# Attention stage of a three-stage kernel: nine tile buffers instead of five, row stores issued by ScalarE, four weight units loaded at the stage's end

## The chip, the cores and the metric

One core of one Trainium2 chip runs the whole program. The metric is device time in microseconds of one execution. A profiled execution gives the trace from which all rows below come; three timed runs give the median.

## The reference

Three layers follow each other. Inputs are float32.

```python
# 1 retention-like attention, batch 8, heads 8, sequence 576, head size 64
ret = (q @ k.T) / 8 * gamma_h ** (i - j) * (i >= j)
x = (ret @ v), laid out as 4608 tokens x 512
# 2 mixture of experts, 8 experts, one expert per token (argmax of x @ w_gate)
h = relu(xe @ w1[e]);  ye = h @ w2[e];  out[mask] = softmax_weight * ye
# 3 dense layer
g = relu(x @ w_in) ** 2;  result = g @ w_out
```

## The kernel before, in words

The kernel works through three stages in an order that is written out by hand; each engine takes its own instructions in that order. The change is in the first stage alone.

**Attention stage.** The 4608 tokens are cut into 36 tiles of 128 tokens. Nine tiles make a pair of batches: tiles 0 to 3 are the four 128-token chunks of one batch, 4 to 7 those of the next, and tile 8 holds the last 64 tokens of both (`kind`). For each tile `load` (L364) brings one array of 128 partitions x 4 x 512 floats (q, k, v and k again: 1 MB; 0.75 MB for every ninth tile) into one of five buffers of the pool `in_p`. In the loop over t, `load(t + 4)` is issued first, so its buffer is the one that tile t-1 has just left. Then, for tile t:

- `scores(t + 1)`: TensorE multiplies k by q (L387), VectorE masks the result into `r` (L393).
- `scale_v(t + 2)`: GpSimd scales v by a table (L374).
- `fold` and `logits` (L476, L467), each in every second tile: the gate's logits of a pair of tiles. ScalarE copies them out of PSUM (L471).
- `out_x(t)`: TensorE multiplies the chunk state `sts` by q (L435; not for the first chunk of a batch; for the ninth tile L428 twice as often) and `r` by v (L439). VectorE scales the sum by the table `tabx` (L447) and transposes it in blocks of 32 into one of three buffers `xr` (L449).
- `state(t)`: TensorE adds v times k to the chunk state (L411), ScalarE copies it to `sts` (L418); the next tile's L435 reads it.

The rows of x go to DRAM (`x_d`) by `put` (L456): four stores of 64 KB each, in pieces of 512 bytes. `out_x(t)` only notes `put` in the list `late`; it is issued in loop t+1, right behind that loop's load, on the same queue (SyncE's, SP):

```python
for t in range(NT):
    ready, late[:] = late[:], []
    if t + 4 < NT:
        load(t + 4)
    ...
    for f in ready:
        f()
```

In the loops t = 12, 18, 24 and 30 SP also issues `load_unit` (L107): one unit of weights of expert 0, 0.5 MB, into the one buffer `stg`. Two loops later `split_unit` makes its high part on ScalarE (L113) and its low part on GpSimd (L115), in a buffer of the pool `w_a`, which has four buffers of 8 KB per partition. These four units are used right behind the attention stage.

Beside this, `group` makes each token's place in its expert's list from the logits of a group of tiles, in steps that `todo` hands out one per loop. After the third group two rows of places are known; GpSimd gathers those 256 rows of x (`lead`, L270), and in the loops 33 and 34 `lead_turn` transposes them on TensorE (L286) and splits them.

**Behind the loop** come `late` (the last tile's `put`), the loads of the units 4 and 5 in halves (L689), and then TensorE's first work of the second stage: `first(0)` (L806 to L808) on the lead rows, `first(1)`, the last logits, `second(0)` (L830), which needs ScalarE's and VectorE's copies of `first(0)` (L812, L813), and so on while the last group's places are made and GpSimd gathers the rest of expert 0's rows (`xs`). Seven more experts and the dense layer follow.

Of the kernel before, what the change touches and what calls it, by code (L numbers as in the profile page):

```python
# [7 lines left out]
F32 = mybir.dt.float32  # L8
F32R = mybir.dt.float32r
# [10 lines left out]
NT = 36  # L20
NE = 8
CAP = 640
CT = CAP // 128
# [2 lines left out]
NF = 16  # L26
FIN = 6
LEAD = 2
MORE = 6
TINY = 2.0 ** -15 * 1.125  # L30
GROUPS = [(0, 8), (8, 16), (16, 24), (24, 30), (30, 36)]
# [18 lines left out]
def body(ctx, tc, att, tab_v, tab_x, masks, wg, ident, pick, cst, wu, wd, out):  # L50
    nc = tc.nc
    vec, act, pe, pool, sp = nc.vector, nc.scalar, nc.tensor, nc.gpsimd, nc.sync

    def scope(stack, name, bufs, space=None, side=None, reuse=None):
        kw = {"space": space, "side": side, "reuse_waits": reuse}
        kw = {k: v for k, v in kw.items() if v is not None}
        return stack.enter_context(tc.tile_pool(name=name, bufs=bufs, **kw))

    const = scope(ctx, "const", 1)
    xs_p = scope(ctx, "xs_p", 1)  # L60
    xf_p = scope(ctx, "xf_p", 2)
    w_a = scope(ctx, "w_a", 4, side="right")
    pools = {}
# [25 lines left out]
    sidx2 = places.tile([128, NE], I32, name="sidx2")  # L89
    lead_idx = places.tile([128, LEAD], I32, name="lead_idx")  # L90
    oh2 = places.tile([128, NT, 2 * NE], BF16, name="oh2")
# [9 lines left out]
    def ring(u):  # L101
        return w_a if u % 8 < 4 else pools["w_b"]


    def load_unit(u, on=None):
        raw = on.tile([128, CT, 4, 128], F32, tag="xs", name="raw").rearrange("p a b c -> p (a b c)")[:, 0:1024] if on else pools["stg"].tile([128, 1024], F32, tag="raw", name="raw")
        sp.dma_start(out=raw, in_=wu[u])  # L107
        return raw

    def split_unit(u, raw, on):  # L110

        w = ring(u).tile([128, 2, 1024], F32R, tag="w", name="w")
        act.activation(out=w[:, 0], in_=raw, func=AF.Copy)  # L113
        w_q[u] = w
        return lambda: on.tensor_tensor(out=w[:, 1], in0=raw, in1=w[:, 0].bitcast(F32), op=ALU.subtract)  # L115
# [211 lines left out]
    rt_ps = scope(chain, "rt_ps", 1, PSUM, side="right")  # L327
    with ExitStack() as es:
        tabs = scope(es, "tabs", 1)
        pools["stg"] = scope(es, "astg", 1)  # L330
        in_p = scope(es, "in_p", 5)
        sp_p = scope(es, "sp_p", 3)
        r_p = scope(es, "r_p", 2)
# [6 lines left out]
        tabx = tabs.tile([128, 5, 4, 128], F32, name="tabx")  # L340
# [10 lines left out]
        def kind(t):  # L351
            g, c = divmod(t, 9)
            if c == 8:
                return None, 4
            return 2 * g + c // 4, c % 4

        def load(t):
            a = in_p.tile([128, 4, 512], F32, tag="in", name="in")
            n = 3 if kind(t)[1] == 4 else 4
            in_t[t] = a  # L360
            if t < 4:
                sp.dma_start(out=a[:, 0:2], in_=att[t, :, 0:2])
            else:
                sp.dma_start(out=a[:, 0:n], in_=att[t, :, 0:n])  # L364
# [33 lines left out]
        def stslot(b, c):  # L398
            return sts[2 + b % 2] if c == 3 else sts[c % 2]
# [20 lines left out]
        def out_x(t):  # L420
            b, c = kind(t)
            q = in_t[t][:, 0].rearrange("p (h n) -> p h n", h=4)
            ps = x_ps.tile([128, 4, 128], F32, tag="x", name="x")
            if c == 4:
                for i in range(2):
                    s = stslot(i, 3)
                    for p in range(4):
                        pe.matmul(  # L428
                            ps[:, p], s[:, p], zq[:, p, i:i + 2].rearrange("p a n -> p (a n)"),
                            start=(p == 0 and i == 0), stop=False, skip_group_check=True,  # L430
                        )
            elif c > 0:
                s = stslot(b, c - 1)
                for p in range(4):
                    pe.matmul(ps[:, p], s[:, p], q[:, p], start=(p == 0), stop=False, skip_group_check=True)  # L435
            for p in range(4):
                for s in range(2):
                    h = 2 * p + s
                    pe.matmul(  # L439
                        ps[64 * s:64 * s + 64, p], vs_t[t][:, 64 * h:64 * h + 64],  # L440
                        r_t[t, s][:, p],
                        start=(c == 0 and p == 0), stop=(p == 3), skip_group_check=True,
                    )
            if t % 2 == 0:
                xp_t[t // 2] = xp_p.tile([128, 4, 256], F32, tag="x", name="x")
            x = xp_t[t // 2][:, :, 128 * (t % 2):128 * (t % 2) + 128]
            vec.tensor_tensor(out=x, in0=ps, in1=tabx[:, c], op=ALU.mult)  # L447
            xr = xr_p.tile([128, 4, 4, 32], F32, tag="xr", name="xr")
            vec.transpose(  # L449
                out=xr.rearrange("q t k j -> q k t j"), in_=x.rearrange("q k (t i) -> q k t i", i=32)  # L450
            )

            def put():
                rows = x_d[128 * t:128 * t + 128, :].rearrange("(t i) (a c) -> a i t c", i=32, a=4)
                for a in range(4):
                    sp.dma_start(  # L456
                        out=rows[a], in_=xr[32 * a:32 * a + 32].rearrange("q t k j -> q t (k j)")
                    )

            late.append(put)  # L460

        def logits(j):
# [108 lines left out]
        def lead_kept(bank):  # L571
# [4 lines left out]
            vec.tensor_scalar(  # L576
                out=kept, in0=kept, scalar1=-1.0, scalar2=128.0 * (LEAD + 1), op0=ALU.mult, op1=ALU.add
            )
# [3 lines left out]
        def lead_rows():  # L582
            f = rt.tile([128, LEAD], F32, tag="lf", name="lf")
            vec.scalar_tensor_tensor(
                out=f, in0=inv[:, NS:NS + LEAD], scalar=128.0, in1=inv[:, 0:LEAD], op0=ALU.mult, op1=ALU.add
            )
            vec.tensor_scalar(out=lead_idx, in0=f, scalar1=-1.0, scalar2=0.0, op0=ALU.add, op1=ALU.max)
            for i in range(LEAD):
                if not lead_s:
# [4 lines left out]
        def lead_turn(i):  # L594
# [3 lines left out]
            act.activation(out=hi, in_=ps, func=AF.Copy)  # L598
            vec.tensor_tensor(out=lo, in0=ps, in1=hi.bitcast(F32), op=ALU.subtract)

        todo = []
        raw = {}
        lead = pools["cw_p"].tile([128, 4, 512], F32R, tag="cw", name="lead")
        lead_x = [
            lead[:, 2 * s:2 * s + 2].rearrange("p s (k n) -> p (s k) n", n=128 * LEAD) for s in range(2)
        ]
# [28 lines left out]
        fold = None  # L635
        for t in range(NT):
            ready, late[:] = late[:], []
            if t + 4 < NT:
                load(t + 4)
            if t in (1, 2, 4):  # L640
                c = {1: 2, 2: 3, 4: 4}[t]
                sp.dma_start(out=tabx[:, c], in_=tab_x[:, c])
            if t == 0:
                sp.dma_start(out=wg2[:, :, 0:NE], in_=wg)
            if t == 2:
                sp.dma_start(out=idn, in_=ident)
            if t == 4:
                sp.dma_start(out=msk[:, 1], in_=masks[:, 1])
                sp.dma_start(out=cf, in_=cst)
            if t == 6:  # L650
                sp.dma_start(out=sel, in_=pick)
            for f in ready:
                f()
            if t % 6 == 0 and 12 <= t < 36:
                raw[t] = load_unit(t // 6 - 2)
            if t + 1 < NT:
                scores(t + 1)
            if t + 2 < NT:
                scale_v(t + 2)
            if fold:  # L660
                fold()
                for g in GROUPS:
                    if g[1] == t - 2:
                        todo += group(*g)
            fold = logits((t - 3) // 2) if t % 2 and t > 2 else None
            out_x(t)
            state(t)
            if t + 1 < NT:
                spread_q(t + 1)
            if NT - 1 - LEAD <= t < NT - 1:  # L670
                lead_turn(t - NT + 1 + LEAD)
            if todo and t < NT - 1:
                todo.pop(0)()
            if t == 8:
                vec.tensor_copy(ub, cf[:, C_U:C_U + 128])
            if t % 6 == 2 and 12 <= t < 36:
                split_unit(t // 6 - 2, raw.pop(t - 2), pool)()
        for f in late:
            f()
        late.clear()  # L680
# [70 lines left out]
    with ExitStack() as es:  # L751
# [225 lines left out]
        raw, made, wide, last_job = {}, [], [], None  # L977
# [33 lines left out]
        for u in range(NU):  # L1011
# [49 lines left out]
            if u + 1 < NU:  # L1061
                first(u + 1, (1,) if u + 1 < MORE else (0, 1))
            if f == 5:
# [4 lines left out]
            if u < NU - FIN:  # L1068
                second(u, range(LEAD if u < MORE else 0, CT))
                if f == 7:  # L1070
# [32 lines left out]
    with ExitStack() as es:  # L1103
# [213 lines left out]
        def tile_of(T, what, a, b):  # L1317
            return first_of[T] + ((7 * a + KEPT.index(b)) // 4 if what == "up" else 14 + 8 * a + b // 2)
# [50 lines left out]
        for m, (T, what, a, b) in enumerate(slots):  # L1369
# [8 lines left out]
            if what == "up":  # L1378
                up(T, a, b, 512 if T else 256)
                if T < 4 and b in (7, 6) and a in (4, 5):  # L1380
                    if (a, b) == (4, 7):
                        load, jobs = prepare(T + 1)
# [10 lines left out]
            t = tile_of(T, what, a, b)  # L1393
# [85 lines left out]
```

## Time and profile before

| | us |
|---|---|
| median of three runs | 1503.47 (1495.17 to 1505.44) |
| profiled execution, device time | 1493.76 |
| its span in the trace | 1492.0 |
| TensorE busy in the span | 1386.8 (93%) |
| VectorE, ScalarE, GpSimd busy | 827.2, 548.2, 356.6 |

The span is the time from the first to the last instruction. Busy times are sums over instructions; TensorE's are modelled and overlap its waits in part. In the rows below a start and a length are in microseconds from the span's start. SPq and ACTq are the DMA issues of SyncE and ScalarE; a name such as `in<-att` is the tile written and the tensor read. A DMA's length in the chain is the time from its issue to its landing.

### The profile page before, as it was taken

The numbers are of one execution on the slowest core, as the hardware profiler recorded it, in microseconds if no ns is written. First come the engines' busy times: TensorE is split into PE (matmuls) and PEld (weight loads), VectorE is DVE, ScalarE is ACT, GpSimd is POOL, SyncE is SP. The second block draws the span as 40 slices with busy tenths as digits, with TensorE's granted clock in tenths as the row PEclk, the third lists the DMA queues.
The fourth block names the chain that finished last, engine by engine and source line by source line (L and its number), as shares of the span: only waits on it lengthen the run. The fifth ranks groups of instructions, "written<-read, shape, count | busy, mean of one in ns | idle before, by whom it ended". The sixth has DMA issues, their size and how long they took to land.

```text
span 1492.0 us, 21533 instructions
## 1 busy us (share of the span) xinstructions
PE 1386.8 (93%) x8121; PEld 1173.8 (79%) x8121; DVE 827.2 (55%) x1512; ACT 548.2 (37%) x1064; POOL 356.6 (24%) x366
## 2 busy tenths in 40 slices
PE   8888998696969798979999999999999999999998
PEld 6777797595949697969797788888888888788887
DVE  5666756383828585857268446534562447435422
ACT  1222243252415253424255344324442444334321
POOL 2232274525251625431123002200030003100000
PEclk9999998797969898979999999999999999999999
DMA  9999745454526565534676666666675666655563
GB/s 316 311 280 301 213 144 189 128 195 141 194 81 231 171 209 183 203 124 170 245 282 249 216 213 223 223 225 207 201 243 203 218 225 226 214 209 197 197 226 113
DMA packets 107712, 311.02 MB, mean 208 GB/s; under 512 B 20430, under 2 KB 55758, under 8 KB 85584
## 3 DMA queue, kind: packets, MB, share of 16 engines
q1 hardware_dynamic: 97152, 288.15, 56.8%
q0 software_dynamic: 9872, 21.15, 4.7%
q8 instruction: 66, 1.08, 0.3%
q14 instruction: 46, 0.38, 0.1%
q10 hardware_dynamic: 576, 0.26, 0.1%
HBM read 257.98 MB, written 52.58 MB: 208 GB/s over the span
## 4 chain that ended last, share of the span: by engine, by line
PE 72%; DMA 12%; issue 10%; POOL 2%; DVE 2%; SPq 1%; ACT 1%; POOLq 0%; DVEq 0%; ACTq 0%
PE b L1146 22%; PE fa L1214 8%; PE fa L1216 8%; PE fa L1215 8%; DMA in<-att 7%; PE l L807 4%; PE l L806 4%; PE l L808 4%; PE acc L830 4%; PE acc L831 4%; PE acc L832 4%; POOL xs L270 1%; DMA wq<-ws_d 1%; DMA tabx<-tab_x 1%; DMA y_d<-y,sidx 1%
## 5 line engine op out<-in xcount | busy, mean ns | idle before, releaser
L1146 PE MATMUL b<-xt,wq 128*128 128x512 f32 (+1 forms) x1296 | 265.1, 362 | 5.0 <-ACT xt L743 2.3
L1146 PEld LDWEIGHTS b<-xt,wq 128*128 128x128 f32 x1296 | 220.9, 188 | 44.3 <-ACT xt L743 3.0
L1214 PE MATMUL fa<-wq,ch 128*128 128x512 f32 x576 | 224.7, 390 | 2.4 <-DVE fo L1226 1.3
L1216 PE MATMUL fa<-wq,cl 128*128 128x512 f32 x576 | 224.6, 390 | 0.2
L1215 PE MATMUL fa<-wq,ch 128*128 128x512 f32 x576 | 224.2, 389 | 0.0
L1204 DVE TENSOR_TENSOR cl<-g,ch 128x512 fp32r<-128x512 f32 (+1 forms) x160 | 108.4, 687 | 174.2 <-ACT ch L1203 171.8
L734 POOL TENSOR_TENSOR xsum<-yf 128x256 f32<-128x256 f32 x80 | 64.2, 813 | 457.5 <-DVE yf L722 390.5
L807 PE MATMUL l<-xt,w 128*128 128x320 f32 (+1 forms) x480 | 155.0, 323 | 18.7 <-issue 18.6
L808 PE MATMUL l<-xt,w 128*128 128x320 f32 (+1 forms) x480 | 154.4, 322 | 17.0 <-issue 17.0
L806 PE MATMUL l<-xt,w 128*128 128x320 f32 (+1 forms) x480 | 154.2, 321 | 13.5 <-issue 13.3
L1203 ACT ACTIVATE ch<-g 128x512 fp32r<-128x512 f32 (+1 forms) x160 | 91.4, 585 | 180.3 <-PE fa L1215 180.3
L270 POOL DMA_INDIRECT xs<-x_d,qidx x140 | 146.1, 1043 | 44.4 <-issue 41.8
L812 ACT ACTIVATE hh<-l 128x320 fp32r<-128x320 f32 (+2 forms) x128 | 55.0, 436 | 259.4 <-PE l L808 116.0
L813 DVE SCALAR_TENSOR_TENSOR hl<-l,hh 128x320 fp32r<-128x320 f32 (+2 forms) x128 | 59.4, 484 | 160.8 <-ACT hh L812 89.5
L831 PE MATMUL acc<-w,hh 128*128 128x512 f32 x320 | 131.3, 410 | 9.7 <-issue 9.6
L830 PE MATMUL acc<-w,hh 128*128 128x512 f32 x320 | 131.9, 412 | 6.4 <-issue 6.2
L832 PE MATMUL acc<-w,hl 128*128 128x512 f32 x320 | 131.2, 410 | 2.6 <-issue 2.2
L1214 PEld LDWEIGHTS fa<-wq,ch 128*128 128x128 f32 x576 | 108.1, 188 | 26.3 <-ACT ch L1203 2.6
L1216 PEld LDWEIGHTS fa<-wq,cl 128*128 128x128 f32 x576 | 108.1, 188 | 24.6 <-DVE cl L1204 2.2
L1215 PEld LDWEIGHTS fa<-wq,ch 128*128 128x128 f32 x576 | 108.1, 188 | 22.3
L807 PEld LDWEIGHTS l<-xt,w 128*128 128x128 f32 x480 | 94.1, 196 | 25.6 <-issue 23.3
L806 PEld LDWEIGHTS l<-xt,w 128*128 128x128 f32 x480 | 93.8, 195 | 22.2 <-issue 20.0
(181 smaller groups left out, 2079.6 us busy)
## 6 DMA issues: line engine op xcount, KB each, us to landing
wq<-ws_d SPq DMA_DIRECT2D x142, 1024.0 KB
raw<-wu SPq DMA_DIRECT2D x62, 512.0 KB
in<-att SPq DMA_DIRECT2D x28, 1024.0 KB
craw<-wd SPq DMA_DIRECT2D x32, 512.0 KB
ws_d<-cw SPq DMA_DIRECT2D x24, 512.0 KB
x_d<-xr SPq DMA_DIRECT2D x144, 64.0 KB
out<-fo SPq DMA_DIRECT2D x32, 256.0 KB
yq<-y_d SPq DMA_DIRECT2D x112, 64.0 KB
```

The lines of the kernel that those rows point to most:

```text
L270: pool.indirect_dma_start(out=xs, out_offset=None, in_=src, in_offset=bass.IndirectOffsetOnAxis(ap=index, axis=0),)
L806: pe.matmul(ps, w[:, 0, k], hi[:, k, cs], start=(k == 0), stop=False)
L807: pe.matmul(ps, w[:, 0, k], lo[:, k, cs], start=False, stop=False)
L808: pe.matmul(ps, w[:, 1, k], hi[:, k, cs], start=False, stop=(k == 3))
L830: pe.matmul(acc[i], hh[:, cs], w[:, 0], start=(f == 0), stop=False)
L831: pe.matmul(acc[i], hh[:, cs], w[:, 1], start=False, stop=False)
L832: pe.matmul(acc[i], hl[:, cs], w[:, 0], start=False, stop=(f == 7))
L1146: pe.matmul(ps, w[:, a, c], xc[T][i, b][c], start=(i in (5, 1, 4) and m == 0), stop=(m == 5), skip_group_check=True,)
L1204: vec.tensor_tensor(out=lo[:, o], in0=s, in1=hi[:, o].bitcast(F32), op=ALU.subtract)
L1214: pe.matmul(acc[i], hi[:, cs], w[:, 0], start=(f == 0), stop=False)
L1215: pe.matmul(acc[i], hi[:, cs], w[:, 1], start=False, stop=False)
L1216: pe.matmul(acc[i], lo[:, cs], w[:, 0], start=False, stop=(f == 15))
```

## The change

The attention stage has nine buffers for its tiles: the four of `w_a` for the tiles with t % 9 < 4, and the five of `in_p` for the rest. The loads of the tiles 4 to 8 are all issued in loop 0, among the small tables, which come there too; from then on `load(t + 8)` is issued in loop t. The four row stores of a tile are issued by ScalarE, at the same place of the order. The weights units 0 to 3 are loaded in the loops 28, 29, 30 and 32, behind the last tile's load (issued in loop 27), into spare space, `stg` and one tile buffer; each is split in the loops 31 to 34, its low part on VectorE.

```diff
+DEEP = 8
+FIRST_UNITS = [28, 29, 30, 32]
...
         def load(t):
-            a = in_p.tile([128, 4, 512], F32, tag="in", name="in")
+            if t % 9 < 4:
+                a = w_a.tile([128, 4, 512], F32R, tag="w", name="in").bitcast(F32)
+            else:
+                a = in_p.tile([128, 4, 512], F32, tag="in", name="in")
...
                 for a in range(4):
-                    sp.dma_start(
+                    act.dma_start(
                         out=rows[a], in_=xr[32 * a:32 * a + 32].rearrange("q t k j -> q t (k j)")
                     )
...
-            if t + 4 < NT:
-                load(t + 4)
-            if t in (1, 2, 4):
-                c = {1: 2, 2: 3, 4: 4}[t]
-                sp.dma_start(out=tabx[:, c], in_=tab_x[:, c])
             if t == 0:
                 sp.dma_start(out=wg2[:, :, 0:NE], in_=wg)
-            if t == 2:
+                load(4)
+                sp.dma_start(out=tabx[:, 2], in_=tab_x[:, 2])
                 sp.dma_start(out=idn, in_=ident)
-            if t == 4:
+                load(5)
+                sp.dma_start(out=tabx[:, 3], in_=tab_x[:, 3])
+                load(6)
                 sp.dma_start(out=msk[:, 1], in_=masks[:, 1])
+                sp.dma_start(out=tabx[:, 4], in_=tab_x[:, 4])
+                load(7)
                 sp.dma_start(out=cf, in_=cst)
+            if t + DEEP < NT:
+                load(t + DEEP)
...
-            if t % 6 == 0 and 12 <= t < 36:
-                raw[t] = load_unit(t // 6 - 2)
+            if t in FIRST_UNITS:
+                u = FIRST_UNITS.index(t)
+                if u == 0:
+                    spare = xs_p.tile([128, CT, 4, 128], F32, tag="xs", name="spare").rearrange("p a b c -> p (a b c)")
+                if u < 2:
+                    raw[u] = spare[:, 1024 * u:1024 * u + 1024]
+                elif u == 2:
+                    raw[u] = stg.tile([128, 1024], F32, tag="raw", name="raw")
+                else:
+                    raw[u] = in_p.tile([128, 4, 512], F32, tag="in", name="raw").rearrange("p a b -> p (a b)")[:, 0:1024]
+                sp.dma_start(out=raw[u], in_=wu[u])
...
-            if t % 6 == 2 and 12 <= t < 36:
-                split_unit(t // 6 - 2, raw.pop(t - 2), pool)()
+            if 31 <= t < 35:
+                split_unit(t - 31, raw.pop(t - 31), vec)()
```

## Rows read from the trace of the kernel before

**Rows 1.** Windows: stretch, its length, each engine's busy time, granted clock, DMA share, GB/s.
```profile
60.00:157.00 97.00, 82.59 (x1235) 70.91 (x1231) 66.42 (x142) 22.87 (x55) 29.13 (x24) 0.98 0.94 292
157.00:175.20 18.20, 16.07 (x223) 13.71 (x220) 13.08 (x34) 5.91 (x13) 6.74 (x6) 1.00 0.70 198
```

**Rows 2.** Waits up to 175.2 us: who waited for what, total, times, longest.
```profile
PE sc L387 <- DMA in<-att: 19.8, 21, 2.5
...
DVE x L447 <- DMA tabx<-tab_x: 8.0, 2, 6.3
```

**Rows 3.** Waits of SP's own queue, up to 175.2 us.
```profile
SPq L456 <- DMA in<-att: 45.3, 30, 2.9
```

**Rows 4.** Timeline of SP's queue around 124 us: start, length, line, DMA, count.
```profile
120.02 0.38 SPq L364 DMA_DIRECT2D in<-att  x1
120.50 3.22 SPq L456 DMA_DIRECT2D x_d<-xr  x4
123.83 0.57 SPq L364 DMA_DIRECT2D in<-att  x1
124.49 1.29 SPq L456 DMA_DIRECT2D x_d<-xr  x2
127.98 0.95 SPq L456 DMA_DIRECT2D x_d<-xr  x2
```

**Rows 5.** DMA view, 0 to 166.4 us: packets, bytes and mean rate of all queues.
```profile
DMA packets 29991, 49.94 MB, mean 300 GB/s; under 512 B 6712, under 2 KB 23313, under 8 KB 26385
```

**Rows 6.** DMA view, 745 to 781 us, GB/s in 40 slices; 1 MB loads alone in the second half.
```profile
GB/s 228 364 391 355 364 405 219 46 0 0 0 128 91 155 118 109 141 128 96 155 246 410 346 373 346 419 391 428 428 428 419 437 428 400 410 391 419 428 355 401
```

**Rows 7.** Timeline of TensorE: scores of tiles 1, 9 and 35, and routing matmuls.
```profile
8.19 1.16 PE L387 MATMUL sc<-in 64*128 64x128 f32 x16 [1.06 <-DMA in<-att]
...
43.04 1.16 PE L387 MATMUL sc<-in 64*128 64x128 f32 x16 [0.23 <-DMA in<-att]
...
151.28 0.46 PE L247 MATMUL rkp<-b,a 128*128 128x80 bf16 x8
...
166.90 1.16 PE L387 MATMUL sc<-in 64*128 64x128 f32 x16
```

**Rows 8.** Chain that ended last, 158 to 191 us: start, length, what.
```profile
158.36 7.76 DMA lead<-x_d,lead_idx
...
166.97 1.09 PE sc L387 x16
168.06 0.37 PE lg L476 x2
168.43 0.89 PE x L435 x8
169.32 1.02 PE x L439 x16
170.35 0.49 PE stp L411 x16
...
172.12 2.05 PE x L428 x16
...
175.20 0.32 PE l L806
...
178.74 0.57 PE lg L467 x8
179.31 0.43 PE acc L830
...
186.84 3.51 DMA xs<-x_d,gidx
```

**Rows 9.** Timeline, ScalarE's queue: two DMA issues of 64 KB each.
```profile
737.96 0.83 ACTq L709 DMA_DIRECT2D yi<-y_d  x2
```

**Rows 10.** Lines up to 330 us: low part of a unit on VectorE and on GpSimd.
```profile
L115 DVE TENSOR_TENSOR w<-raw,w 128x1024 fp32r<-128x1024 f32 x17 | 20.4, 1202 | 3.5 <-ACT w L113 2.4 <-issue 1.0
...
L115 POOL TENSOR_TENSOR w<-raw,w 128x1024 fp32r<-128x1024 f32 x4 | 9.7, 2430 | 8.9 <-ACT w L113 8.9
```

**Rows 11.** Timeline of VectorE behind the last tile: the last transpose.
```profile
176.77 0.71 DVE L449 STREAM_TRANSPOSE xr<-x 128x512 f32<-128x512 f32 x1
```

More of the change, by code (lines that the diff above doesn't have):

```diff
@@ L329, in body @@
         tabs = scope(es, "tabs", 1)
-        pools["stg"] = scope(es, "astg", 1)
+        stg = scope(es, "astg", 1)
         in_p = scope(es, "in_p", 5)
@@ L599, in lead_turn @@
             vec.tensor_tensor(out=lo, in0=ps, in1=hi.bitcast(F32), op=ALU.subtract)
-        todo = []
-        raw = {}
+        todo, raw = [], {}
         lead = pools["cw_p"].tile([128, 4, 512], F32R, tag="cw", name="lead")
```

## The prediction
> **What bounds the kernel now.** I read the windows first. From 60 to 157 us TensorE is busy 82.6 of 97 us, the DMA engines 94% of it, VectorE 66 and ScalarE 23 [rows 1]: DMA is the fullest resource of this stage. The waits say the same from TensorE's side: scores waited 21 times for a tile, 19.8 us in all, and VectorE lost 8.0 us to a late table [rows 2]. The reader should then ask whether the DMA engines lack speed or lack work. Rows 4 answer in part. SP issues a load at 120.02, four stores, the next load at 123.83, two stores, and then stands still until 127.98, with nothing of its own to wait for but its place in the queue: eight transfers are out, and the oldest, the load of 120.02, has just landed. SP lost 45.3 us to such stalls [rows 3]. [...] Up to 166.4 us, about when the last tile lands, all queues moved 49.94 MB at 300 GB/s [rows 5]; 1 MB loads alone go at about 410 GB/s (second half of the slices in [rows 6]). A tile (1.05 MB in, 0.26 MB out) takes 4.37 us at 300 GB/s, and its load 2.56 us at 410.
>
> The end to watch is the start of the second stage's matmuls, 175.20 us [rows 8]. Behind it the program is the same, so I carry every microsecond of that end through to the whole time; no row argues that a later stage waits for something that starts at a fixed time.
>
> **What TensorE needs if no tile is late.** From the pieces in the chain [rows 8] a tile costs 1.09 + 0.89 + 1.02 + 0.49 = 3.49 us, and half of 0.37 + 0.57 for the logits: 3.96. Tile 1's scores start at 8.19 [rows 7]; 34 tiles further is 134.6 us. Seven of these tiles are first chunks and lack the 0.89: -6.2. Three ninth tiles have 2.05 for 0.89 + 0.49: +2.0. Four groups of routing matmuls, the largest piece of which is 0.46 [rows 7], I estimate at 1.25 each: +5. That puts the scores of tile 35 at 143.6, where before has 166.90. From there to the end it was 175.2 - 166.9 = 8.3, so the stage would end at 152.
>
> **The change, part by part.**
>
> *Nine buffers, stores off SP's queue.* SP then holds only loads; a load waits for tile t-1 to be left, as before, but eight tiles ahead instead of four, and SP's eight places hold loads alone. The stalls of [rows 3] go as a brake on loads, and the late table's 8.0 us too, since the tables now stand among the first loads. Between two bounds: at the present 300 GB/s nothing is won but the bytes that move (rival C); at best the loads are never late and TensorE's own 152 holds. I take 152 as the base, because the stall of [rows 4] leaves the engines with one load in hand at times and the new order leaves them with several. At 410 GB/s a tile's 1.31 MB is 3.20 us, under 3.96.
>
> *Late next: the stores.* Nine tiles (9.2 MB) and the tables (1.7 MB), 10.9 MB, are asked for at once: 26.6 us at 410. The stores of tile 0 come at about 13 us and meet that backlog from another queue. No row has stores beside loads on two queues. The nearest is the lead gather: two transfers on GpSimd's queue took 7.76 us beside loads and stores on SP's, where a gather with that queue idle took 3.51 [rows 8]; 4.25 more for two, so each waited about 2.1, nearly one 1 MB load. Four stores at 2.56 + 0.16 each make 10.9 us per tile while the backlog lasts. Eight places on ScalarE's queue are two tiles of stores: the stores of tile 3 then hold ScalarE until those of tile 1 are through, at 13 + 2 x 10.9 = 35; behind them on ScalarE stands the state copy (L418) of tile 4, for which tile 5 waits on TensorE from about 27: 8 us. By about 42 us the backlog is gone, for loads come only as fast as tiles are left; a second such step would make it 14. Bounds 0 (stores slip in between a load's packets) and 14; I take **8**, nearer to the gather's row than to none.
>
> *Stores on ScalarE.* Two 64 KB issues take 0.83 us [rows 9], four 1.66 per tile; ScalarE is busy 22.9 of 97 us [rows 1], so 1.66 of 3.96 fits. They stand behind the state copy of their own tile and before that of the next, which needs TensorE's next 3.96 us: nothing in the steady state. At the end they show. The last transpose ends at 176.77 + 0.71 = 177.48 [rows 11]; then four issues to 179.14, then two copies of `first(0)` of about 0.4 each, to about 180.1, while `second(0)` started at 179.31 [rows 8]: **0.9** (bounds 0 and 1.9).
>
> *The four units.* Low parts go from GpSimd, 4 x 2.43, off the path, to VectorE, 4 x 1.20 = 4.8 us [rows 10], all in the last four loops. VectorE had 13.08 of 18.2 us there [rows 1]; with 4.8 it has 17.9 in about 17: it is the bound, and the last x comes late. The last logits have some room behind `first(1)`. I take **2** (bounds 0 and 4.8). The four high parts on ScalarE move into the same loops, beside its stores; I include them in that. Their 2.1 MB leave the path of the last tile, which matters only in rival C. SP's other entries (one logits store per group) stay; unit 3's load waits for tile 31 and has nothing behind it that is due. GpSimd is only relieved.
>
> Sum: 152 + 8 + 0.9 + 2 = 163 against 175.2, **12 us less**. The profiled execution's 1493.76 becomes 1482; the median of the three runs stands 9.7 us above it, so the median forecast is 1503.5 - 12 = **1491**.
>
> [...]
>
> **Rivals.**
>
> *B, no store waits and TensorE sets the pace.* The stage ends at 152 + 2.9 = 155, or 153 with no cost at the end: 20 to 22 us less, 1482 to 1483. For: 410 GB/s and DMA idle gaps. Against: the gather's row.
>
> *C, the DMA engines stay the bound.* At 300 GB/s the last tile needs the same bytes less 2.1 MB of units: 47.8 MB, 159 us plus the 8.8 that before took from 166.4 to the end, plus 2.9: 171, 4 us less, 1499. For: the 94% share in [rows 1]. Against: SP's stalls.
>
> *D, slower: ScalarE held by its stores, at an unchanged DMA pace.* Tile 9 starts 14 us later, at 57. From 43.04 to 166.90 before took 123.9 for 26 tiles [rows 7], of which the four units are 2.1 MB / 300 = 7 and the wait for the lead rows about 1.5: 4.44 each, so 115.4 more, 172.4, plus 8.3 + 2.9 = 184: 8 us slower, 1512. It decides where the tiles behind tile 9 still need more than about 4.1 us each: 57 + 26 x 4.1 + 11.2 = 175.
>
> **Chances.** Forecast 0.45 (1485 to 1497), B 0.27, C 0.17, D 0.08, something not seen 0.03. Range 1476 to 1506: B's best with a run-to-run spread like that of the three runs below it, C whole with the same above it, and D outside. Of this kernel about 1%, 15 us, can be told from no change. Faster by over 1%: B nearly whole and a fifth of the forecast, 0.35. Slower by over 1%: half of D, some of what I have not seen, and the upper bounds coming together, 0.09. Within 1%: 0.56.
>
> **What would show it.** Right: TensorE's waits for `in<-att` behind 45 us near zero; tile 35's scores at 150 to 154; SP's stalls now on loads and harmless; ScalarE's queue waiting in its store issues between 20 and 45 us, and the state copy late there; VectorE full in the last four loops. Wrong: scores still waiting for tiles at the end (C); no store waits at the start (B); store stalls on ScalarE after 60 us (D); or the second stage longer than the 1316.8 us that it has now from 175.2 to the span's end.

## The result, and the profile after

The changed kernel took 1518.77 us (median of 6 runs, 1516.22 to 1527.5) against 1502.98 us for the kernel before on the same chip (6 runs): a ratio of 1.0131, 95% interval 1.0095 to 1.0166. It is about 1.3% slower. The ratio and its interval come from the fast runs alone, so they differ from the quotient of the two medians, 1.0105. The forecast was 1491, range 1476 to 1506, so the sign and the range were both wrong; "slower by over 1%" had been given 0.09.

I read the profile after in the order of the prediction. First the stretches of [rows 1], with the second one ending where the second stage's matmuls now start:

```profile
60.00:157.00 97.00, 86.03 (x1165) 73.46 (x1163) 63.51 (x133) 17.49 (x48) 19.80 (x19) 0.90 0.89 301
157.00:183.64 26.64, 26.03 (x386) 22.41 (x382) 24.55 (x55) 11.38 (x23) 6.29 (x6) 1.00 0.52 137
```

TensorE looks busier than before (86.03 against 82.59 us) and yet got less done (1165 matmuls against 1235): its granted clock, as a share of the full one, fell from 0.98 to 0.90. The DMA engines moved 301 GB/s where 292 had been. The load-ahead did not turn into speed.

Then the waits up to the stage's end (who waited for what, total, times, longest), against [rows 2]:

```profile
POOL vs L379 <- DMA in<-att: 37.6, 13, 5.5
ACT ls L476 <- DMA x_d<-xr: 21.8, 5, 9.6
ACT sts L423 <- DMA x_d<-xr: 18.9, 4, 6.4
...
PE sc L392 <- DMA in<-att: 7.9, 3, 4.2
DVE x L452 <- DMA tabx<-tab_x: 7.3, 1, 7.3
```

Two rows are new: ScalarE's logit copies (`ls`) and state copies (`sts`) stood 40.7 us behind stores of rows (the time to issue them included), a wait that before did not have at all. TensorE's own wait for tiles fell from 19.8 to 7.9, all of it before 60 us. The late table, which the prediction had written off, still cost 7.3. Behind 60 us TensorE waited for no tile. These are its own waits from 60 to 184 us:

```profile
PE lg L481 <- ACT ls L476: 7.3, 4, 2.7
PE x L433 <- ACT zq L374: 3.4, 2, 3.0
...
PE x L440 <- ACT sts L423: 0.2, 1, 0.2
```

All three wait for something that ScalarE makes (`zq` is its copy of q for a ninth tile). Before had, in the same stretch, 14.8 us for tiles:

```profile
PE sc L387 <- DMA in<-att: 14.8, 15, 2.5
```

SP's own queue, against the 45.3 us of [rows 3]:

```profile
SPq L369 <- DMA x_d<-xr: 52.8, 11, 9.0
SPq L369 <- PE stp L416: 21.0, 7, 4.3
...
SPq L369 <- DMA in<-att: 16.1, 3, 6.4
```

L369 is the load of a tile. It stood 52.8 us for *stores* (`x_d<-xr`) that another engine had issued. Only the 21.0 us for `stp`, the tile that has to be left first, is what the prediction expected. The chain that ended last shows the two queues taking turns (start, length, what):

```profile
12.05 6.28 DMA x_d<-xr
18.35 0.35 SPq L369
...
45.83 8.85 DMA x_d<-xr
...
57.23 8.86 DMA x_d<-xr
66.11 0.31 ACTq L461
66.46 0.44 ACTq L461
66.94 10.36 DMA x_d<-xr
77.38 0.31 ACTq L461
...
79.29 0.39 ACT ls L476
79.69 0.04 issue
79.73 0.69 PE lg L481 x2
80.42 2.05 PE x L440 x8
82.47 1.93 PE x L444 x16
...
110.68 8.67 DMA in<-att
119.37 0.31 ACTq L461
```

At 18.35 a load goes out the moment a store has landed. At 119.37 it is the other way round: a store on ScalarE goes out when a load has landed. Between 46 and 77 three stores follow one another, each about 9 to 10 us long, and behind the third, at 79.29, stands the logit copy for which TensorE's next matmuls wait. The instruction records of this trace name what ties them: the transfers of SP's and ScalarE's queues share eight completion counters (semaphores 100, 102 to 106, 108 and 109). Up to 175 us, 63 transfers of SP and 132 of ScalarE take the eight strictly in turn, and of these 195 all but the first eight wait on the counter that they take, 121 by themselves and 66 by an instruction ahead of them: each waits until the one eight before it has landed. GpSimd's 241 transfers in the same trace take eight others (111 to 118). The kernel does not ask for these counters by name; they come with the compiled program, and no run shows a limit of the chip in them. A tile is one load and four stores, so eight transfers are 1.6 tiles here, with five buffers or nine and whichever of the two engines issues.

The end of the stage moved from 175.13 us [rows 8] to 183.64, and the first matmul on gathered tokens from 190.40 to 201.84, 11.4 us later. The profiled span grew by 24.2 (1492.0 to 1516.2). The other 12.8 lie in later stages; the last section comes back to them.

### The profile page after: what moved, and what is told of

Same layout as the page of the kernel before. It is cut to its first block, busy times and chain, and to the rows that moved or that the text cites. A ratio compares the mean times of both kernels' runs of the same rounds, so it can differ in the third digit from the quotient of the medians.

```text
span 1516.2 us, 21528 instructions
## 1 busy us (share of the span) xinstructions
PE 1395.0 (92%) x8121; PEld 1181.3 (78%) x8121; DVE 832.6 (55%) x1516; ACT 545.8 (36%) x1064; POOL 343.1 (23%) x362
## 3 DMA queue, kind: packets, MB, share of 16 engines
q1 hardware_dynamic: 76416, 278.70, 52.8%
## 4 chain that ended last, share of the span: by engine, by line
PE 73%; issue 10%; DMA 9%; DVE 3%; POOL 2%; ACT 1%; ACTq 1%; SPq 0%; DVEq 0%; POOLq 0%
PE b L1161 22%; PE fa L1229 8%; PE fa L1231 8%; PE fa L1230 8%; DMA x_d<-xr 5%; PE l L821 4%; PE l L823 4%; PE l L822 4%; PE acc L845 4%; PE acc L847 4%; PE acc L846 4%; DMA in<-att 2%; POOL xs L272 1%; DMA y_d<-y,sidx 1%; PE x L444 1%
## 5 line engine op out<-in xcount | busy, mean ns | idle before, releaser
L293 POOL DMA_INDIRECT y_d<-y,sidx x40 | 43.2, 1080 | 287.1 <-ACT y L856 265.0
L822 PEld LDWEIGHTS l<-xt,w 128*128 128x128 f32 x480 | 93.7, 195 | 17.2 <-issue 14.9
```

The source lines that it names most:

```text
L822: pe.matmul(ps, w[:, 0, k], lo[:, k, cs], start=False, stop=False)
```

## The experiments

Three causes were held against each other. **Theory 1**: stores and loads wait for one another through the shared count, and ScalarE, held by a store, makes copies late. **Theory 2**: stores starve beside loads, whatever the count. **Theory 3**: the work moved to the end. The kernels ran on several chips, each beside the kernel before on its own chip; the ratio is to that. "Stage end" is the first matmul on the lead tokens, "tile 9" the start of its scores, both from one profile. Three profiles of the kernel before, on three chips, had the stage end at 175.13, 173.83 (c4) and 171.71 (e2, where 173 to 176 had been expected), and two of the changed kernel at 183.64 and 185.94: differences of the stage end under some 4 us are not read. Tile 9 of these three came at 43.04, 43.22 and 41.95, and of the changed kernel's two at 46.54 and 46.79.

| kernel | transfers per tile in the shared count | tile 9 | stage end | from tile 9 to end | ratio, 95% interval |
|---|---|---|---|---|---|
| before | 5 | 43.04 | 175.13 | 132.1 | 1 |
| changed | 5 | 46.54 | 183.64 | 137.1 | 1.0131 [1.0095, 1.0166] |
| a1_sp_stores | 5 | 53.47 | 178.06 | 124.6 | 1.0113 [1.0019, 1.0207] |
| a2_act_only | 5 | 50.64 | 179.13 | 128.5 | 1.0141 [1.0029, 1.0253] |
| a3_pool_stores | 1 | 42.87 | 158.85 | 116.0 | 0.9930 [0.9875, 0.9986] |
| a4_pool_lows | 5 | 45.98 | 193.71 | 147.7 | 1.0253 [1.0144, 1.0363] |
| b1_after | 5 | 46.79 | 185.94 | 139.2 | 1.0112 [1.0090, 1.0134] |
| b2_pair_act | 3 | 42.43 | 167.81 | 125.4 | 1.0022 [1.0004, 1.0039] |
| b3_pool_five | 1 | 45.21 | 164.31 | 119.1 | 0.9924 [0.9902, 0.9946] |
| b4_pool_nine | 1 | 42.30 | 158.26 | 116.0 | 0.9880 [0.9861, 0.9899] |
| c1_double_act | 9 | 56.13 | 227.05 | 170.9 | 1.0418 [1.0382, 1.0454] |
| c2_pool_loads | 4 (stores) | 59.52 | 184.46 | 124.9 | 1.0121 [1.0091, 1.0151] |
| d1_vec_copies | 5 | 48.98 | 190.41 | 141.4 | 1.0131 [1.0087, 1.0175] |
| d2_pool_loads_vec | 4 (stores) | 60.22 | 191.79 | 131.6 | 1.0138 [1.0047, 1.0230] |

**The parts alone.** a1 is the changed kernel with the stores back on SP; a2 is the kernel before with the stores on ScalarE and nothing else.

```diff
 a1:  -                    act.dma_start(        (changed kernel, L461)
      +                    sp.dma_start(
 a2:  -                    sp.dma_start(         (kernel before, L456)
      +                    act.dma_start(
```

> The changed kernel with the row stores back on SyncE's queue; nine buffers, the late units and VectorE's low parts stay. Theory 1: the loss comes from ScalarE's issuing the stores: a store there waits until the eighth transfer before it, in the program's order over both queues, has landed, and holds ScalarE's state and logits copies. Then the time falls to about that of the kernel before, 1495 to 1507 us, and the copies (sts, ls) wait no more for x_d. Theory 2: loads that run eight tiles ahead starve the stores, whichever queue issues them: 1512 to 1522, as the changed kernel. Theory 3: the work moved to the stage's end (VectorE's low parts, stores ahead of the first copies) is the loss: 1512 to 1520.

> The kernel before with one part of the change alone: its row stores are issued by ScalarE; five buffers, units and low parts as before. Theory 1: slower than before by most of the loss, 1510 to 1525 us, with ScalarE's copies waiting 30 to 50 us for x_d. Theory 2: loads run only four tiles ahead, so little is starved: within 4 us of before, 1499 to 1507. Theory 3: only the last tile's stores ahead of the first copies count: 1 to 3 us over before, 1504 to 1506.

Neither half wins anything; for a1 theory 1 had expected about the time of before, and the ratio of 1.0113 missed that. With nine buffers and the stores on SP, the stage from tile 9 on took 124.6 us, 7.5 less than before, but the opening, where nine loads and all tables are asked for ahead of the first stores, took 10.4 more, and the stage ended at 178. With the stores on ScalarE and five buffers it ended at 179. That loss too lies in the opening, 7.6 us, and from tile 9 on the stage took 3.6 less than before; ScalarE's copies there already waited for stores, 54.5 us:

```profile
ACT ls L471 <- DMA x_d<-xr: 28.9, 5, 11.9
ACT sts L418 <- DMA x_d<-xr: 25.6, 5, 7.5
```

So the wait on ScalarE comes with the queue, not with the buffers. Behind tile 9 each half alone is faster than before, and only the two together are slower (137.1 against 132.1); why they do not add up was not tested.

**The stores on GpSimd, the low parts on GpSimd.**

```diff
 a3:  -                    act.dma_start(        (changed kernel, L461)
      +                    pool.dma_start(
 a4:  -                split_unit(t - 31, raw.pop(t - 31), vec)()
      +                split_unit(t - 31, raw.pop(t - 31), pool)()
```

> The changed kernel with the row stores issued by GpSimd, whose transfers have a queue and a count of their own. Theory 1: neither SyncE nor ScalarE is held by a store; loads fill their own eight places: the stage ends 15 to 25 us earlier than in the changed kernel and the time is 1488 to 1502 us; if stores are served one packet for one of the loads, GpSimd's scaling of v is late in the first 45 us. Theory 2: the stores are starved as much as on ScalarE's queue: 1512 to 1522. Theory 3: 1512 to 1520, since the end is unchanged but for 1 us.

> The changed kernel with the four units' low parts back on GpSimd, in the same late loops. Theory 1: the end alone is shorter, by 1 to 3 us: 1514 to 1519 us. Theory 2: the same. Theory 3: VectorE's 4.8 us at the end are the loss: 1503 to 1511.

a3 turned the change into a gain: stage end 158.85, no wait of ScalarE for a store, 5.0 us of TensorE waiting for tiles. a4 gained nothing and ended its stage later than either profile of the changed kernel. Its trace shows most of that: from 172.97 to 181.92 GpSimd made three of the low parts and two scalings almost without a break, and beside them one small compare on VectorE, which takes 0.22 us in the three earlier groups of a4, took 8.37:

```profile
173.62 8.37 DVE L506 TENSOR_TENSOR eq<-lgt,mx 128x48 f32<-128x48 f32 x1
```

The mask for which the scores of tile 35 waited stands behind it on VectorE, and these scores started at 183.37. So a4 by itself is no clean test of VectorE's low parts. a3 is: it keeps them on VectorE and gains, so theory 3 falls as the cause.

**How many transfers a tile is.** b1 is the changed kernel again. b2 sends the rows of two tiles together, four stores of 128 KB; c1 cuts each store in two. The bytes, the queue and the issuing engine stay, and each piece of a row is still 512 B.

```diff
 b2:  -            xr = xr_p.tile([128, 4, 4, 32], F32, tag="xr", name="xr")
      +            if t % 2 == 0:
      +                xr2[0] = xr_p.tile([128, 8, 4, 32], F32, tag="xr", name="xr")
      +            xr = xr2[0]
      ...
      +            if t % 2 == 0:
      +                return
      -                rows = x_d[128 * t:128 * t + 128, :]...
      +                rows = x_d[128 * t - 128:128 * t + 128, :]...
 c1:  -                    act.dma_start(out=rows[a], in_=xr[32 * a:32 * a + 32]...)
      +                    for h in range(2):
      +                        act.dma_start(out=rows[a][:, 2 * h:2 * h + 2],
      +                                      in_=xr[32 * a:32 * a + 32, 2 * h:2 * h + 2]...)
```

> The changed kernel once more, as the measure for the other three on this chip. Every theory: slower than the kernel before by 1 to 2%; attention stage (start of the second stage's first matmul) at 180 to 190 us in its profile. How far it is from 183.6 is how far one look of the stage can be trusted.

> The changed kernel, but the rows of two tiles leave in one set of four stores of 128 KB, so that a tile costs 1 + 2 transfers on the two queues where it cost 1 + 4; bytes, 512 B packets and the issuing engine are the same. Theory 1 (a transfer waits for the eighth before it on SP's and ScalarE's queues together, so that eight are 1.6 tiles of work): eight transfers become 2.7 tiles, ScalarE's and SP's waits for stores shrink by half or more, and the stage ends at 160 to 172 us instead of 184; 10 to 20 us less than the changed kernel. Theory 2 (the packets of the loads starve the stores, whatever the count): the bytes and packets wait as before, the stage ends at 180 to 188.

> The changed kernel with each store of rows cut in two (eight of 32 KB for a tile where there were four of 64 KB); bytes, 512 B packets, queue and issuing engine are the same. Theory 1 (each transfer of the two queues waits for the eighth before it): a tile is now 9 transfers, so that eight are less than a tile, and every load waits for stores of the tile just finished: stage end beyond 205 us, and 25 us or more over the changed kernel. Theory 2 (packets and bytes): stage end 184 to 192, since only ScalarE's issue time grows by some 1.7 us a tile.

With 3, 5 and 9 transfers a tile the stage ended at 167.8, 183.6 to 185.9 and 227.1. That is the order that theory 1 gave, and near its numbers; theory 2 had 180 to 188 and 184 to 192. One part of the expectation missed: ScalarE's waits for stores in b2, 26.6 us against 40.9 in b1, did not shrink by half; SP's loads' did, 25.5 against 67.7. ScalarE's waits for stores in c1, up to 185 us, against 40.7 us in the changed kernel:

```profile
ACT ls L478 <- DMA x_d<-xr: 73.4, 11, 11.9
ACT sts L423 <- DMA x_d<-xr: 37.2, 7, 6.0
```

and its stretch from 60 to 120 us, columns as in [rows 1]:

```profile
60.00:120.00 60.00, 45.60 (x552) 38.58 (x553) 29.58 (x59) 8.63 (x25) 9.38 (x9) 0.86 0.79 272
```

The DMA engines had a fifth of their time free (share 0.79) while ScalarE and SP waited for transfers to land: the limit in this run is the number of transfers, not the engines' speed. That number acts in two ways, which b1, b2 and c1 do not separate: by the count, and by ScalarE's time for issuing, which from tile 9 to the stage's end was 55.5 us for 112 stores in b1, 29.9 for 56 in b2 and 100.0 for 225 in c1. c2, below, keeps the issuing and changes the count.

**Queue or buffers.** b3 is the kernel before with the stores on GpSimd's queue, one word changed; b4 repeats a3 beside it.

```diff
 b3:  -                    sp.dma_start(         (kernel before, L456)
      +                    pool.dma_start(
```

> The kernel before with one edit: the stores of rows on GpSimd's queue (five buffers, units as before). Theory 1: SP's transfers no longer have stores among the eight, the stalls of its queue go, and the stage ends at 160 to 168 us, 8 to 15 us less than before, without any of the nine buffers; the gain of the kernel with nine buffers and stores on GpSimd is mostly that of the queue. If the nine buffers are what counts: 172 to 178, the time of before.

> The changed kernel with its stores on GpSimd's queue, once more, beside the five-buffer one. Theory 1: stage end near 159 us, total 10 to 15 us under the kernel before and some 25 under the changed kernel. If the earlier run was an accident: stage end at 175 or later and a total like the changed kernel's.

The queue alone brings the stage from about 174 to 164.3; nine buffers, the earlier tables and the later units bring 6 us more, now that nothing else holds them. b4, at 0.9880 of before, is the fastest kernel here. From 60 to 120 us:

```profile
60.00:120.00 60.00, 59.98 (x903) 51.44 (x901) 47.51 (x94) 13.99 (x37) 47.84 (x74) 1.00 1.00 368
```

TensorE is busy 59.98 of the 60 us, at a granted clock of 1.00, and the DMA engines move 368 GB/s. GpSimd is busy 47.84 us, most of it issuing stores (77.0 us for 140 of them up to 158 us), and has the room.

**What the prediction had assumed.** c2 leaves the stores on ScalarE and lets GpSimd issue the tile loads, so that tile loads and stores no longer count together. SP's small tables still count with the stores.

```diff
 c2:  -                sp.dma_start(out=a[:, 0:n], in_=att[t, :, 0:n])
      +                pool.dma_start(out=a[:, 0:n], in_=att[t, :, 0:n])
```

> The changed kernel with its stores left on ScalarE, but the 1 MB tile loads issued by GpSimd, so that loads and stores no longer count together: what the prediction assumed of the change. Theory 1: ScalarE's eight are then two tiles of stores, its waits for stores fall to a few us, and the stage ends at 158 to 168 us. Theory 2 (stores beside loads on another queue starve, and ScalarE is held by that): the packets meet as before, ScalarE is held as before, 178 to 188. Against both: GpSimd's scaling of V now stands behind a load that waits for its buffer, which could cost some us of its own.

The stage ended at 184.46, which speaks for theory 2 as it was written down. The table shows two halves. From tile 9 on it took 124.9 us, 12 to 14 less than the changed kernel, with as many stores issued by ScalarE (112, in 55.3 us). So that gain is not one of issuing; what c2 changed is who issues the loads, and with it what the stores count with. The opening took 59.5, 13 more, and there the slow stores of theory 2 show. ScalarE's stores met the backlog of nine loads, one of 64 KB took 16.62 us to land, and the store eight transfers behind it could not go out before 44.82 (chain, then timeline of ScalarE's queue). The four stores took 8.16 us to issue for such waits, and ScalarE stood 10.44 us before the state copy behind them:

```profile
28.18 16.62 DMA x_d<-xr
...
36.97 8.16 ACTq L461 DMA_DIRECT2D x_d<-xr  x4
45.23 0.78 ACT L423 ACTIVATE sts<-stp 64x256 f32<-64x256 f32 x2 [10.44 <-DMA x_d<-xr]
```

So the opening of c2 has both: stores that land late, and the count of eight that turns them into a hold.

**Which of the two waits.** d1 is the changed kernel with the copies L423 and L476 on VectorE, d2 is c2 with the same.

```diff
 d1, d2:  -            act.activation(out=s[o, :, o], in_=acc[o], func=AF.Copy)
          +            vec.tensor_copy(s[o, :, o], acc[o])
          -            act.activation(out=ls, in_=ps, func=AF.Copy)
          +            vec.tensor_copy(ls, ps)
```

> The changed kernel with the state copies and the logit copies of the attention stage on VectorE instead of ScalarE, so that nothing that TensorE waits for stands behind a store on ScalarE; every transfer stays where it was. If the hold of ScalarE is what costs: the stage ends at 160 to 170 us, though SP's loads still wait for stores. If the loads that wait for stores to land are what costs: 178 to 188, tiles late on TensorE instead of copies. VectorE takes some 1.0 us a tile more and could add a few us of its own.

> The version with the tile loads issued by GpSimd and the stores by ScalarE, with the same copies on VectorE. If stores that starve beside the first loads cost only through ScalarE's hold: tile 9 starts near 43 us instead of 59.5 and the stage ends at 158 to 166. If the late stores cost by themselves (buffers of rows not free): tile 9 stays beyond 50 and the stage ends at 172 or later.

Neither got shorter (190.4 and 191.8; d1's is outside both of its expected ranges), so moving these copies to VectorE does not cure the stage. d1 does not settle which wait costs, though: ScalarE still made `zq` behind its stores, and TensorE now waited for VectorE's copies, which stand behind other work there, far more than the few us that were expected:

```profile
PEld x L440 <- DVE sts L423: 22.8, 24, 2.0
...
PE x L440 <- DVE sts L423: 14.3, 22, 1.5
```

The changed kernel's own trace settles it better: behind 60 us TensorE stood for ScalarE's results and for no tile. SP's loads did wait for stores (37.2 us behind 60 us), but with nine buffers that did not reach TensorE there.

d2 shows that slow stores also cost without ScalarE's copies: tile 9 stayed at 60.2, because VectorE's transposes waited for a free row buffer, which a store had not yet left (13.5 us in 2 waits).

**Pairs on GpSimd, and the size of packets.** c3 is b4 with b2's pairs; c4 and e2 are the kernel before for its profile; e1 is b4 with a gap in the row buffer.

```diff
 e1:  -            xr = xr_p.tile([128, 4, 4, 32], F32, tag="xr", name="xr")
      +            xr = xr_p.tile([128, 4, 5, 32], F32, tag="xr", name="xr")[:, :, 0:4]
```

> The version with nine buffers and stores on GpSimd's queue, with the rows of two tiles in one set of four stores. A candidate for the fastest. Theory 1: the count no longer limits (TensorE sets the pace there at 158), so pairing gives little: 156 to 160, within 4 us of the unpaired one. If GpSimd's issue time or its queue still costs: 150 to 155.

> The kernel before once more, for a profile on this chip: stage end at 172 to 176 us by every theory. How far it is from 175.2 is how far one look can be trusted.

> The version with nine buffers and stores on GpSimd's queue, with a gap of 128 bytes behind each 512 B piece of the transposed rows in SBUF. If the packets become 512 B and the count is what matters: stage end stays at 157 to 163 us and the total 10 to 16 us under the kernel before. If the 2 KB packets are what matters: stage end 170 or later and no gain over the kernel before. If the packets stay at 2 KB the run tells nothing.

c3's stage ended at 157.79, as theory 1 had it, and its total was 0.9956 [0.9940, 0.9972]: worse than unpaired. Its first matmul on gathered tokens came at 180.30, 22.5 us after the stage's end, where b4 needed 15.7. The rows of the last two tiles leave together there, which fits the delay; no run separates it. e1 (0.9884 [0.9836, 0.9932], stage end 157.05) kept its packets at about 2 KB (4.54 MB in 2225 packets from 60 to 130 us), so it only confirms b4. In the DMA view, 60 to 130 us (packets, MB, share of 16 engines), the stores of the changed kernel (b1) on ScalarE's queue are

```profile
q10 hardware_dynamic: 7995, 3.65, 18.2%
```

and those of b4 on GpSimd's, with the few other transfers of that queue,

```profile
q0 software_dynamic: 2313, 4.72, 18.3%
```

3650 KB in 7995 packets is about 460 B each, 4720 in 2313 about 2 KB, and the engines spent 18.2 / 3.65 = 5.0 against 18.3 / 4.72 = 3.9 points of share for each MB. How much of GpSimd's gain comes from its own count and how much from larger packets stays open: no run here separates the two.

## Why the prediction was wrong

**What failed: stores on ScalarE, put at "nothing in the steady state".** The loss lies behind tile 9. From tile 9's scores to tile 35's TensorE does the same work in the kernel before, the changed kernel and b4 (1577 to 1581 matmuls; columns as in [rows 1]):

```profile
43.04:166.90 123.86, 106.12 (x1577) 91.22 (x1577) 83.32 (x181) 29.45 (x72) 39.44 (x33) 0.99 0.94 296
46.54:174.48 127.94, 114.51 (x1581) 98.00 (x1577) 87.05 (x182) 26.09 (x69) 29.22 (x28) 0.92 0.85 283
42.30:148.17 105.87, 104.89 (x1580) 90.44 (x1576) 88.76 (x182) 27.57 (x70) 84.72 (x128) 1.00 0.90 327
```

The changed kernel takes 22.1 us more than b4, where the stores are off ScalarE. Of these, 12.5 are idle time of TensorE (13.43 against 0.98), practically all before matmuls that wait for ScalarE's `ls`, `zq` and `sts`, and 9.6 are the same matmuls at a lower clock (0.92 against 1.00), for which the prediction has no term. The stores had been put at nothing because four issues fit into ScalarE's time. What it left out is that a store there waits for the eighth transfer before it, SP's loads included, and ScalarE's copies wait behind the store.

**The misreading behind it.** [Rows 3] and [rows 4] showed SP stop at eight transfers, and I took the eight for places of SP's queue; they are counters that SP and ScalarE share. So "SP's eight places hold loads alone" was false (SP's loads waited 52.8 us for stores on the other queue), and so was "eight places on ScalarE's queue are two tiles of stores". The base of 152 rested on the first. Its condition, that no tile is late, did come about behind 60 us, and even so the base was not reached, for the term above. TensorE's estimate behind the base was some 6 us short but of the right kind: with the stores out of the shared count (a3, b4, e1) the stage ended at 157.05 to 158.85, at TensorE's own pace.

**The 8 us for starved stores.** In the changed kernel tile 9 came 3.5 us late (46.54 against 43.04 [rows 7]), not 8. That the shared count also throttles the loads which should have starved them would explain it, and c2 fits: where tile loads and stores count apart, the opening cost 16.5 us, above the upper bound of 14.

**The 2.9 us at the end** (0.9 for stores ahead of the first copies, 2 for VectorE's low parts) came out near in sum and wrong in its parts. From the scores of tile 35 to the first matmul on gathered tokens it was 190.40 - 166.90 = 23.5 us before and 201.84 - 174.48 = 27.4 after, 3.9 more. With the late low parts on VectorE but the stores on SP (a1) it was 25.2, 1.7 more where 2 had been given; with the stores on ScalarE alone (a2) it was 26.7, 3.2 more where 0.9 had been given. The two overlap. Part of it shows in the chain, a low part directly ahead of the last tile's scaling, which an unlanded store had held:

```profile
181.73 2.16 DMA x_d<-xr
...
184.26 1.22 DVE w L117
185.48 0.61 DVE x L452
186.11 0.72 DVE xr L454
186.86 0.31 ACTq L461
187.21 1.52 DMA x_d<-xr
188.74 0.39 ACT hh L827
```

**The rivals.** D named ScalarE held by its stores, which is what happened, and gave a stage end of 184 and 1512 us; the stage ended at 183.64. The number is right partly by accident: D put the whole loss into the opening, tile 9 at 57 and the old pace behind it, while the runs have tile 9 at 46.5 and a slower pace to the end (137.1 us against 132.1). Its sign that stores would stall ScalarE "after 60 us" was seen (the chain from 57 to 79; 35.8 of the 40.7 us lie behind 60). C, the DMA engines as the bound, falls with c1 and b4: 272 GB/s with a fifth of the time free in c1, and 368 GB/s in b4 from 60 to 120 us, so the 300 that C took as the limit was none. B, TensorE as the pace, is what b4 became, at 158 instead of 155. What I should have weighed is the chance of D: a store in front of ScalarE's copies was a known wait, and only the guess at the count kept it at 0.08.

**Issuing from another engine.** Moving the same stores from SP to ScalarE made the kernel before slower (a2, 1.0141; 4 us in the stage, at the edge of what one profile tells), moving them to GpSimd made it faster (b3, 0.9924; 10 us). In this program the choice of the issuing engine thus changed more than the time of issuing: with what lies behind the issue, it did harm in one place and good in the other, and the measurement decides.

**From the stage to the total.** That every microsecond of the stage's end is carried through holds within 4 us on two of the chips, if the end is taken at the first matmul on gathered tokens. From there to the end of the span it was 1185.3 us for the kernel before (c4) on one, and 1189.0 for the changed kernel (b1), 1184.9 (b2), 1186.2 (b3) and 1187.3 (b4) on the other. On the chip of the prediction it did not hold: 1301.6 before and 1314.4 after. The prediction's own sign for that was seen: from the stage's end to the span's end it took 1332.6 us, not 1316.8. The lead tokens' matmul at 175.2, which I watched, misses the rows that leave late; b2 shows it, with a stage 6 us shorter than before's (167.81 against 173.83) and the same time to gathered tokens (189.09 against 188.87), so no gain.

## What to carry to other kernels

Before a transfer is moved to another engine's queue, find out what its waits count: a stall after a fixed number of transfers, eight here, may be a shared counter. Here neither a second engine on the same count nor more buffers bought anything, while fewer and larger transfers took back most of the loss and a queue with a count of its own gained. Ask what stands behind each transfer on the engine that would issue it: here ScalarE's copies, for which TensorE waits, stood behind late stores, while GpSimd had slack. Put a wait at nothing only after naming what it waits for. Watch the end at the point where the moved data is next read, not at the nearest matmul.

## What the runs showed of the hardware

Beside a late copy the changed kernel shows two losses. From 76 to 80 us TensorE was busy 1.53 of 4.00 us and stood 2.46 us for the logit copy; from 80 to 85 its granted clock was 0.50:

```profile
76.00:80.00 4.00, 1.53 (x17) 1.23 (x16) 3.79 (x8) 0.68 (x3) 0.88 (x1) 0.90 1.13 368
80.00:85.00 5.00, 5.00 (x42) 4.40 (x41) 1.08 (x3) 0.34 (x1) 0.00 (x0) 0.50 0.79 259
```

and in the chain above the pieces of a tile at L440 and L444 took 2.05 and 1.93 us where [rows 8] have 0.89 and 1.02. Whether the idle time brings the lower clock was not tested. From tile 9's scores to tile 35's TensorE was busy 114.51 us for the work that took 106.12 before (rows above): 8.4 us more at 0.92 against 0.99, while its idle time fell from 17.7 to 13.4. So on this chip the stretch grew by the clock, not by idle time. On the two other chips it was both: 113.14 us busy (b1, 0.93) against 108.26 (c4, 0.97), and 16.9 idle against 14.1.

The same program was granted a mean clock of 0.89 on one chip and of 1.00 on another. The kernel before, from 200 to 740 us, on the chip of the prediction:

```profile
200.00:740.00 540.00, 470.64 (x2372) 408.91 (x2370) 327.34 (x576) 197.60 (x340) 223.09 (x214) 0.89 0.53 176
```

and on the chip of c4:

```profile
200.00:740.00 540.00, 534.31 (x2996) 480.60 (x2995) 401.20 (x740) 254.35 (x493) 254.16 (x251) 1.00 0.67 228
```

Its span was 1492.0 there and 1374.2 here, 118 us apart with nothing changed in the kernel. The clock is only part of it: behind the first matmul on gathered tokens TensorE was busy 1221.3 us there and 1175.0 here, and idle 80.3 and 10.3.

The 12.8 us that the first chip's two profiles show behind that point are not the clock's. Before and after, from the first matmul on gathered tokens to the end:

```profile
190.40:1492.00 1301.60, 1221.30 (x5840) 1033.97 (x5840) 701.80 (x1236) 503.79 (x959) 304.01 (x317) 0.95 0.58 198
201.84:1516.20 1314.36, 1220.24 (x5840) 1034.04 (x5840) 699.47 (x1235) 502.53 (x958) 300.44 (x318) 0.95 0.57 196
```

TensorE was busy as long, at the same clock, and idle 94.1 us instead of 80.3. In most of that idle time TensorE waited for nothing that the profile shows ("issue": 66.9 and 83.2 us between 200 and 745), so its cause stays open. On the other chips it all but vanishes: the changed kernel's span (b1) exceeded before's (c4) by 18.9 us, 15.2 of them up to the gathered tokens.
